# Folding the router weights two groups at a time, with the transposes of six groups behind the folds

## The chip, the cores and the metric

The kernel runs on one core of a Trainium2 chip. The metric is the device time of one execution in microseconds; smaller is better. Before the change the median of three runs is 1796.62 us (1796.1 to 1796.91).

## The reference, cut to what matters

```python
# S = 2048 tokens, D = 1024, H = 32 heads, E = 8, dk = 128
g = sigmoid((x * gate_w).sum(-1, keepdims=True))
a = attention(x, wqkv, wo)            # 32 heads, softmax, output projection
# b: a router picks one of 64 experts per token and head
q  = einsum("nd,dhc->nhc", x, w_q)    # w_q: D x 32 x 256
s1 = einsum("nhd,ed->nhe", q[..., :128], k1)
s2 = einsum("nhd,ed->nhe", q[..., 128:], k2)
e  = argmax(s1) * 8 + argmax(s2)
b  = sum over heads of gelu(x . u[e]) * v[e]
out = g * a + (1 - g) * b
```

Only the largest score of each half is asked for, so the kernel never forms `q`. It folds `w_q` with the keys into one small matrix per head and half: with `d` the model dimension, `w_q[d, head, half] . (k[e] - k[0])` for the seven differences e = 1 to 7. This folding ("router weights") is what the change touches.

## The kernel before, in words

**Stages.** The first 360 us of the span compute the queries and keys (K and Q) of the attention as a matrix product of `wqkv` and `x`, in two passes of eight units each (units 0 to 7, then 8 to 15; `KC` is 8). Units 0 and 8 are a plain product in four PSUM banks (`plain_banks`, `plain_mm`, `plain_group`, `plain_evac`); they are written out by hand and do not go through `unit(u)`. Units 1 to 7 and 9 to 15 are a Strassen-Winograd product: seven products P1 to P7 of 12 matmuls each (`product`), in the order P1, P5, P6, P2, P7, P3, P4. Every number is split into a high and a low part, and a product takes three matmuls for each of its four slices. ACT makes the high parts (`hi_of`, L138), DVE the low parts (`lo_of`, L141), the sums of the products (`add`, L519) and the sums of the weights (`w_sum`, L226) for the next unit. `evac` stores a finished K or Q block as `hi` and `lo`; what it leaves in `late` (the squares on ACT, L249, and the stores to DRAM that POOL issues) runs at the next `run_late`, which the next `evac` calls. So the square that is the last reader of a PSUM bank comes one `evac` after its block.

**The order of the work** is the order in which the code is written (a manual schedule): each engine executes its instructions in program order, and an instruction waits on semaphores for its operands and for the buffer it writes.

**Folding.** `w_q` is cut into 8 groups of 4 tiles, 32 tiles in all. One tile, one "visit", takes 4 matmuls (128 by 32 weights `kpad`, 512 columns moving, line L345); four visits of a group add up in one PSUM bank, 6 for even groups and 7 for odd ones (`bank_at(6 + gi % 2)`). `VISITS` says how many visits stand at the end of which unit, behind P4 (`fold(u)`). When a group's fourth visit is issued, ACT copies the bank to a buffer (L349, the `u7` buffer that the unit's P7 sum uses too); later four PE transposes (L360) turn it, ACT copies the result (L363, `u7` again) and POOL issues its store to `WPD` in DRAM. In the kernel before, `fold_t` does these last steps in the next unit: after P2 in units 1, 2, 8, 9 and 10 (`u % KC <= 2`), after P5 in the others. `load_wqs` loads the tiles of the next unit's visits on the SP queue: two into the `wqt` buffers, a third into an `x8` buffer.

**Banks.** The products P1 to P7 take banks 0 to 5 in turn. The plain units 0 and 8 hold their four blocks in banks 7, 0, 1 and 2; the block in bank 7 is the one with weight half 0 and column half 0.

Of the kernel before, what the change touches and what calls it, by code (L numbers as in the profile page):

```python
# [19 lines left out]
KC = D // 128  # L20
# [11 lines left out]
def gated_mha_peer_kernel(ctx, tc, xT, wqkv, wv, wo, wq, k12, ug, v, out):  # L32
# [44 lines left out]
    def dma(dst, src, queue=nc.sync):  # L77
        a, b = (ap.bitcast(F32) if ap.dtype == F32R else ap for ap in (dst, src))
        return queue.dma_start(a, b)
# [37 lines left out]
    def bank_at(i):  # L117
        return ps1.tile([128, 512], F32, name=f"bk{i}")
# [18 lines left out]
    def hi_of(parts, src):  # L137
        nc.scalar.activation(parts[0], src, AF.Copy)  # L138

    def lo_of(parts, src):  # L140
        nc.vector.tensor_tensor(out=parts[1], in0=src, in1=parts[0].bitcast(F32), op=OP.subtract)  # L141
# [63 lines left out]
    def load_w(u):  # L205
        t = wr.tile([128, 2, KC, 128], F32, name="wraw")
        for w in range(2):
            dma(t[:, w], wqkv[w * 8 + CHUNK[u]].rearrange("p (k m) -> p k m", k=KC))
        wraw[u] = raw_quarters(t)
# [9 lines left out]
    def w_sum(u, name):  # L219
        r = wraw[u]  # L220
        a, b, op, out = dict(
            S1=("A21", "A22", OP.add, None), S2=("S1", "A11", OP.subtract, "A11"),
            S3=("A11", "A21", OP.subtract, None), S4=("A12", "S2", OP.subtract, "A21"))[name]
        a, b = r[a], r[b]
        r[name] = r[out] if out else wr.tile([128, HC, 128], F32, name=name, bufs=1)
        nc.vector.tensor_tensor(out=r[name], in0=a, in1=b, op=op)  # L226

    def w_hi(u, name, src=None):
        hi_of(w_place(name), wraw[u][src or name])

    def w_lo(u, name, src=None):
        lo_of(AW[name], wraw[u][src or name])
# [9 lines left out]
    def run_late():  # L242

        for f, *a in late:
            f(*a)
        late.clear()
# [6 lines left out]
    def free_held():  # L253
        for parts, src in held:
            lo_of(parts, src)
        held.clear()

    def evac(which, c, n, src, ps, hold=False):
        hi, lo = (ev.tile([128, 512], F32R, name=part) for part in ("hi", "lo"))
        hi_of((hi, lo), src)  # L260
        run_late()
        if hold:
            held.append(((hi, lo), src))
        else:
            lo_of((hi, lo), src)
        late.append((squares, ps, src, which, c, n))
        for i, t in zip(QK_PARTS[which], (hi, lo)):
            late.append((dma, QKD[which][128 * c:128 * c + 128, i, n * 512:(n + 1) * 512], t, nc.gpsimd))
# [28 lines left out]
    def product(name):  # L297
        ps = bank_at(prod_no[0] % 6)
        prod_no[0] += 1
        a, b = (m[f] for m, f in zip((AW, X), FACTORS[name]))  # L300
        for k in range(HC):
            for i, j in ((0, 0), (0, 1), (1, 0)):
                nc.tensor.matmul(ps, a[i][:, k, :], b[j][:, k, :],  # L303
                                 start=(k == 0 and i == j == 0), stop=(k == HC - 1 and i == 1))
        return ps
# [4 lines left out]
    wq_t = {}  # L310

    def load_wq(n, third):
        t = x8.tile([128, HC, 512], F32, name="x8") if third else None
        for half in range(2):
            wq_t[n, half] = (t[:, 2 * half:2 * half + 2] if third else
                             wqp.tile([128, 2, 512], F32, name="wqt", bufs=4))
            dma(wq_t[n, half], wq[n // 4, n % 4][:, half * 1024:(half + 1) * 1024].rearrange("p (a m) -> p a m", a=2))

    VISITS = {0: 2, 1: 2, 2: 3, 3: 3, 4: 3, 5: 3, 7: 2, 8: 2, 9: 3, 10: 3, 11: 3, 12: 3}

    def load_wqs(u):
        for i in range(VISITS.get(u, 0)):
            load_wq(wq_no[0], i == 2)
            wq_no[0] += 1

    def kpad_diffs():
# [2 lines left out]
            nc.gpsimd.tensor_tensor(out=kpad[:, :, i, 7 * i:7 * i + 7], in0=kraw[:, :, 1:],  # L329
                                    in1=kraw[:, :, 0:1].to_broadcast([128, 2, 7]), op=OP.subtract)  # L330

    fold_ps, fold_no, wq_no, pending = [], [0], [0], []

    def fold(u):

        for _ in range(VISITS[u]):
            n = fold_no[0]
            fold_no[0] += 1
            gi, i = divmod(n, 4)
            if i == 0:  # L340
                fold_ps[:] = [bank_at(6 + gi % 2)]
            ps, = fold_ps
            t = wq_t.pop((n, 0)), wq_t.pop((n, 1))
            for quad in range(4):
                nc.tensor.matmul(ps[32 * quad:32 * quad + 32, :], kpad[:, quad % 2, i, :],  # L345
                                 t[quad // 2][:, quad % 2, :], start=(i == 0), stop=(i == 3))
            if i == 3:
                wt = ev.tile([128, 512], F32, name="u7", bufs=1)
                nc.scalar.activation(wt, ps, AF.Copy)  # L349
                pending.append((gi, wt))  # L350
        load_wqs(u + 2 if u == KC - 3 else u + 1)

    def fold_t():
        if not pending:
            return
        gi, wt = pending.pop(0)
        b, dh = divmod(gi, 2)
        pt = bank_at(6 + gi % 2)
        for dc in range(4):
            nc.tensor.transpose(pt[:, dc * 128:(dc + 1) * 128], wt[:, dc * 128:(dc + 1) * 128], ident)  # L360
        wt2 = ev.tile([128, 512], F32, name="u7", bufs=1)[:, :448].rearrange(
            "p (a q r) -> p a q r", a=4, q=4)
        nc.scalar.activation(wt2, pt.rearrange("p (a q r) -> p a q r", a=4, q=4)[:, :, :, :28], AF.Copy)  # L363
        dma(WPD[:, 4 * dh:4 * dh + 4, 112 * b:112 * b + 112], wt2.rearrange("p a q r -> p a (q r)"),
            nc.gpsimd)
# [82 lines left out]
    hooks = {}  # L448
# [41 lines left out]
    def unit(u):  # L490
        p, c, v = u // KC, CHUNK[u], u + 1
        n0 = TOK0[p] // 512
        seven = v < NUNIT and v != KC
        turns = (dict(P2=("S1+", "S3+", "A11"), P7=("S1", "S2+", "S2"), P3=("S4+", "A12"), P4=("S3", "S4"))
                 if u % KC == 1 else
                 dict(P1=("S1+", "S3+", "A11"), P5=("S1", "S2+"), P6=("S2", "S4+"), P2=("A12",),
                      P7=("S3",), P3=("S4",), P4=("A22",)))

        def ready(name):
            todo = turns.get(name, ()) if seven else ()  # L500
            for part in todo:
                if part[-1] == "+":
                    w_sum(v, part[:-1])
                else:
                    w_hi(v, part)
            free_held()
            for part in todo:
                if part[-1] != "+":
                    w_lo(v, part)

        def hook(name):
            for f, *a in hooks.pop((u, name), []):
                f(*a)

        def place(name):
            return ev.tile([128, 512], F32, name=name, bufs=1)

        def add(out, a, b):
            nc.vector.tensor_tensor(out=out, in0=a, in1=b, op=OP.add)  # L519

        p1 = product("P1")
        c1 = place("c1")
        nc.scalar.activation(c1, p1, AF.Copy)
        run_late()
        hook("P1")
        ready("P1")
        p5 = product("P5")
        if u % KC > 2:
            fold_t()
        hook("P5")  # L530
        ready("P5")
        p6 = product("P6")
        u2, u4 = place("u2"), place("u4")
        hook("P6")
        add(u2, c1, p6)
        add(u4, u2, p5)
        ready("P6")
        if v + 1 < NUNIT and v + 1 != KC:
            load_w(v + 1)
        p2 = product("P2")  # L540
        if u % KC <= 2:
            fold_t()
        hook("P2-")
        add(c1, c1, p2)
        evac(0, c, n0, c1, p2, True)
        hook("P2")
        ready("P2")
        p7 = product("P7")
        hook("P7-")
        u7 = place("u7")  # L550
        add(u7, u4, p7)
        add(u2, u2, p7)
        evac(1, c, n0 + 1, u7, p7, True)
        hook("P7")
        ready("P7")
        p3 = product("P3")
        hook("P3-")
        add(u4, u4, p3)
        evac(0, c, n0 + 1, u4, p3, True)
        hook("P3")  # L560
        ready("P3")
        p4 = product("P4")
        add(u2, u2, p4)
        evac(1, c, n0, u2, p4, True)
        if u in VISITS:
            fold(u)
        hook("P4")
        ready("P4")

# [26 lines left out]
    for u in range(1, KC):  # L596
        unit(u)
# [97 lines left out]
    run_late()  # L695
    rwl, rw = pools
    Wp = [(wh_[i][:, k, :], wl_[i][:, k, :]) for i in range(2) for k in range(HC)]
    assert not hooks and fold_no[0] == 32 and not pending

    blk = const.tile([128, 4], F32, name="blk")  # L700
    pr = const.tile([128, KC], F32, name="pr")
# [797 lines left out]
    for h in range(H):  # L1499
        base = h * NT  # L1500
        g, j = divmod(h, 4)
# [20 lines left out]
    for k in range(2 * KC):  # L1522
        c = slice(k % 2 * D // 2, (k % 2 + 1) * D // 2)
# [310 lines left out]
```

## Time and profile before

| | |
|---|---|
| median of 3 runs | 1796.62 us |
| the profiled execution | 1797.13 us |
| its span in the profile | 1795.4 us |
| PE busy | 1789.1 us |
| DVE, ACT, POOL busy | 1505.6, 1302.5, 264.4 us |
| matmuls of the visits (L345) | 256 records, 32.1 to 301.6 us, 31.4 us busy |
| transposes (L360) | 32 records, 4.8 us busy |

PE is TensorE's matmul stream, PEld its weight loads, DVE is VectorE, ACT is ScalarE, POOL is GpSimd, SP issues DMAs. A row of the timeline gives the start in us from the span's beginning, the duration, the engine, the line, the operation, what it writes and reads, how many in a row, and in brackets how long the engine was idle before it and what ended that. Matmuls overlap, so the time that one takes in a stream is read from start to start, not from its duration.

### The profile page before, as it was taken

Reading aid. Unit: us, or ns where it says so; the run is one execution under the profiler, and the core shown is the slowest. Engines: PE = TensorE matmul, PEld = TensorE weight load, DVE = VectorE, ACT = ScalarE, POOL = GpSimd, SP = SyncE. Lnnn points to the kernel's source line nnn. Section 1 sums busy time; section 2 is a strip of 40 time slices with the busy share of each in tenths; the row PEclk is TensorE's granted clock in tenths of the full one; section 3 lists DMA queues with packets and bytes.
Section 4 is the critical chain, followed back from the end, with each engine's and each line's share of the span. In section 5 each row is a group of like instructions: output and inputs, shape, how many; then the busy total and the mean of one; then the engine's idle time right before and its main releaser. Section 6 shows DMA issues by size and latency. Waiting matters only on the chain.

```text
span 1795.4 us, 26107 instructions
## 1 busy us (share of the span) xinstructions
PE 1789.1 (100%) x9911; PEld 1093.8 (61%) x9911; DVE 1505.6 (84%) x1295; ACT 1302.5 (73%) x1702; POOL 264.4 (15%) x395
## 2 busy tenths in 40 slices
PE   9999999999999999999999999999999999999999
PEld 7777777888888644444444444444444444447887
DVE  8866876779977898989899899989989898887874
ACT  6545544522343599999999999999999999994221
POOL 1222222244101101011101111110110111000000
PEclk9999999999999999999999999999999999999999
DMA  7887687360267668889889888988987897877541
GB/s 285 310 313 268 226 310 290 131 223 14 83 220 248 225 147 197 178 182 201 174 196 195 198 186 199 206 180 196 194 205 176 181 206 163 207 190 278 226 158 59
DMA packets 118736, 360.13 MB, mean 201 GB/s; under 512 B 16176, under 2 KB 49216, under 8 KB 95888
## 3 DMA queue, kind: packets, MB, share of 16 engines
q0 software_dynamic: 29520, 152.63, 37.1%
q1 hardware_dynamic: 87784, 203.57, 35.6%
q10 hardware_dynamic: 1304, 2.24, 0.3%
q8 instruction: 79, 1.29, 0.3%
q14 instruction: 49, 0.40, 0.1%
HBM read 171.99 MB, written 72.36 MB: 136 GB/s over the span
## 4 chain that ended last, share of the span: by engine, by line
PE 95%; DMA 2%; issue 1%; ACT 1%; DVE 0%; SPq 0%; POOL 0%; ACTq 0%; POOLq 0%; DVEq 0%
PE ring L1342 28%; PE o L1363 25%; PE bk L303 15%; PE pa L968 7%; PE bk L968 6%; PE bk L729 5%; PE bk L987 2%; PE bk L291 2%; PE bk L345 2%; DMA accd<-P 1%; PE pa L1586 1%; ACT P L1352 1%; PE ring L1376 0%; DMA rb<-rd 0%; PE bk L193 0%
## 5 line engine op out<-in xcount | busy, mean ns | idle before, releaser
L1352 ACT ACTIVATE P<-ring 128x1024 f32<-128x1024 f32 (+2 forms) x1029 | 910.0, 986 | 17.7 <-PE ring L1342 2.7
L1392 DVE TENSOR_TENSOR acc<-acc,P 128x2048 f32<-128x2048 f32 x230 | 527.0, 2291 | 34.4 <-ACT P L1352 14.6
L1363 PE MATMUL o<-P,V 128*32 128x512 f32 x3840 | 464.8, 599 | 0.0
L1342 PE MATMUL ring<-Q,K 98*128 98x512 f32 x1024 | 272.6, 408 | 0.5 <-ACT P L1352 0.5
L1342 PEld LDWEIGHTS ring<-Q,K 98*128 98x128 f32 x1024 | 182.3, 188 | 145.1 <-ACT P L1352 83.7
L1342 PE MATMUL ring<-z,z 98*128 98x512 f32 x1016 | 269.5, 407 | 0.0
L1342 PEld LDWEIGHTS ring<-z,z 98*128 98x128 f32 x1016 | 181.0, 188 | 141.4 <-ACT P L1352 76.6
L1392 DVE TENSOR_TENSOR vhl<-vhl,P 128x2048 f32<-128x2048 f32 x104 | 238.3, 2291 | 17.8 <-ACT P L1352 8.9
L1363 PEld LDWEIGHTS o<-P,V 128*32 128x32 f32 x3840 | 99.1, 109 | 222.6 <-issue 214.1
L1385 POOL DMA_DIRECT2D accd<-P x81 | 71.0, 877 | 821.3 <-ACT P L1352 412.9
L303 PE MATMUL bk<-xh,A 128*128 128x512 f32 x336 | 81.9, 394 | 0.0
L303 PE MATMUL bk<-xh,S 128*128 128x512 f32 x336 | 81.0, 392 | 0.0
L303 PE MATMUL bk<-xl,S 128*128 128x512 f32 x336 | 79.7, 390 | 0.0
L1390 DVE TENSOR_TENSOR acc<-P,P 128x2048 f32<-128x2048 f32 x22 | 50.4, 2292 | 31.7 <-ACT P L1352 31.7
L303 PEld LDWEIGHTS bk<-xh,A 128*128 128x128 f32 x336 | 62.3, 188 | 22.0 <-issue 3.4
L138 ACT ACTIVATE hi<-u 128x512 fp32r<-128x512 f32 x42 | 26.5, 632 | 65.3 <-DVE u L519 35.2
L303 PEld LDWEIGHTS bk<-xl,S 128*128 128x128 f32 x336 | 63.0, 188 | 13.0
L303 PEld LDWEIGHTS bk<-xh,S 128*128 128x128 f32 x336 | 62.6, 188 | 12.9
L968 PE MATMUL pa<-woh,acc 128*128 128x512 f32 x216 | 70.0, 390 | 0.0
L1352 ACT ACTIVATE accd<-ring 128x1024 f32<-128x1024 f32 (+2 forms) x64 | 62.3, 1033 | 0.1
L519 DVE TENSOR_TENSOR u<-u,bk 128x512 f32<-128x512 f32 x70 | 46.6, 683 | 5.3 <-DMA wpd<-u 4.5
L1395 DVE TENSOR_TENSOR acc<-acc,accd 128x2048 f32<-128x2048 f32 x22 | 50.3, 2285 | 0.0
(326 smaller groups left out, 2284.4 us busy)
## 6 DMA issues: line engine op xcount, KB each, us to landing
accd<-P POOLq DMA_DIRECT2D x81, 1024.0 KB, 9.9
wqt<-in_wq SPq DMA_DIRECT2D x48, 512.0 KB
wraw<-in_wqkv SPq DMA_DIRECT2D x28, 512.0 KB
acc<-acc POOLq DMA_DIRECT2D x19, 512.0 KB, 11.8
kd<-hi POOLq DMA_DIRECT2D x32, 256.0 KB, 3.6
kd<-lo POOLq DMA_DIRECT2D x32, 256.0 KB, 5.8
qd<-hi POOLq DMA_DIRECT2D x32, 256.0 KB, 3.6
qd<-lo POOLq DMA_DIRECT2D x32, 256.0 KB, 3.6
```

The costliest lines, as they stand in the source:

```text
L291: nc.tensor.matmul(b0[w, n], AW[PLAIN[w, ki]][a][:, k, :], X[f"B{ki + 1}{n + 1}"][b][:, k, :], start=first, stop=last)
L303: nc.tensor.matmul(ps, a[i][:, k, :], b[j][:, k, :], start=(k == 0 and i == j == 0), stop=(k == HC - 1 and i == 1))
L519: nc.vector.tensor_tensor(out=out, in0=a, in1=b, op=OP.add)
L729: nc.tensor.matmul(ps, x_part(a, t // 4, kc)[:, tok], b, start=first, stop=last)
L968: nc.tensor.matmul(ps, self.a[a][i][:, k, :], self.b[b][j][k], start=(not first and k == 0 and i == j == 0), stop=(k == HC - 1 and i == 1))
L1342: on_ring(nc.tensor.matmul(ring[:, i, :], K[:98, kt * 128:(kt + 1) * 128], Q[:98, qc * 512:(qc + 1) * 512], start=True, stop=True), i)
L1352: on_ring(nc.scalar.activation(P[h, kt][:, q0 * 512:(q0 + m) * 512].rearrange("p (a m) -> p a m", a=m), ring[:, i:i + m, :], AF.Exp, scale ...
L1363: nc.tensor.matmul(O[h][32 * qc:32 * qc + 32, :], Vt[g][:, kt, 32 * j:32 * j + 32], p[:, qc * 512:(qc + 1) * 512], start=(kt == 0), stop=( ...
L1385: nc.gpsimd.dma_start(ACCD[h], P[h, kt], accum_op=OP.add)
L1390: nc.vector.tensor_add(ACC[h], P[h, 0], P[h, kt])
L1392: nc.vector.tensor_add(ACC[h], ACC[h], P[h, kt])
L1395: nc.vector.tensor_add(ACC[h], ACC[h], ACCD[h])
```

## The change

`VISITS` now names a group (a to h) for each visit, and each half of the groups is folded in the order aa, ab, abb, bcc, ccd, ddd: the visits of two groups are open at the same time, in banks 6 and 7. The number of visits at the end of each unit is the same as before, and so is the number of loads. A group that is finished while more visits follow in the same unit (a, b, c in the first half, e, f, g in the second) is marked; its four transposes stand directly behind these visits (`fold_turn(True)`), ahead of the next unit's P1. The last `evac` of the unit, which the visits followed before, now stands behind them, and the copy of the transposed group and its store (`fold_out`) behind that `evac`. Groups d and h, which end with the last visit of a unit, are transposed in the next unit after P5. No instruction is added or removed.

```diff
-    VISITS = {0: 2, 1: 2, 2: 3, 3: 3, 4: 3, 5: 3, 7: 2, 8: 2, 9: 3, 10: 3, 11: 3, 12: 3}
+    VISITS = {0: "aa", 1: "ab", 2: "abb", 3: "bcc", 4: "ccd", 5: "ddd",
+              7: "ee", 8: "ef", 9: "eff", 10: "fgg", 11: "ggh", 12: "hhh"}
+    ALL = "".join(VISITS[u] for u in sorted(VISITS))
...
-    fold_ps, fold_no, wq_no, pending = [], [0], [0], []
+    fold_ps, fold_no, wq_no, pending = {}, [0], [0], []

     def fold(u):

-        for _ in range(VISITS[u]):
-            n = fold_no[0]
+        for left in range(len(VISITS[u]))[::-1]:
+            g = ALL[fold_no[0]]
+            gi, i = "abcdefgh".index(g), ALL[:fold_no[0]].count(g)
             fold_no[0] += 1
-            gi, i = divmod(n, 4)
             if i == 0:
-                fold_ps[:] = [bank_at(6 + gi % 2)]
-            ps, = fold_ps
-            t = wq_t.pop((n, 0)), wq_t.pop((n, 1))
+                fold_ps[gi] = bank_at(6 + gi % 2)
+            ps = fold_ps[gi]
+            t = wq_t.pop((4 * gi + i, 0)), wq_t.pop((4 * gi + i, 1))
             for quad in range(4):
                 nc.tensor.matmul(ps[32 * quad:32 * quad + 32, :], kpad[:, quad % 2, i, :],
                                  t[quad // 2][:, quad % 2, :], start=(i == 0), stop=(i == 3))
             if i == 3:
                 wt = ev.tile([128, 512], F32, name="u7", bufs=1)
                 nc.scalar.activation(wt, ps, AF.Copy)
-                pending.append((gi, wt))
+                pending.append((gi, wt, left > 0))
         load_wqs(u + 2 if u == KC - 3 else u + 1)

-    def fold_t():
-        if not pending:
+    turned = []
+
+    def fold_turn(at_once):
+        if not pending or pending[0][2] != at_once:
             return
-        gi, wt = pending.pop(0)
-        b, dh = divmod(gi, 2)
+        gi, wt, _ = pending.pop(0)
         pt = bank_at(6 + gi % 2)
         for dc in range(4):
             nc.tensor.transpose(pt[:, dc * 128:(dc + 1) * 128], wt[:, dc * 128:(dc + 1) * 128], ident)
+        turned.append((gi, pt))
+
+    def fold_out():
+        if not turned:
+            return
+        gi, pt = turned.pop()
+        b, dh = divmod(gi, 2)
         wt2 = ev.tile([128, 512], F32, name="u7", bufs=1)[:, :448].rearrange(
...
@@ unit(u) @@
         p5 = product("P5")
-        if u % KC > 2:
-            fold_t()
+        fold_turn(False)
+        fold_out()
...
         p2 = product("P2")
-        if u % KC <= 2:
-            fold_t()
...
         p4 = product("P4")
         add(u2, u2, p4)
-        evac(1, c, n0, u2, p4, True)
         if u in VISITS:
             fold(u)
+            fold_turn(True)
+        evac(1, c, n0, u2, p4, True)
+        fold_out()
```

Three places show the new order. The names: `bk6_453` is a tile in PSUM bank 6, `u7_813` one in the buffer `u7`, `wqt` and `x8` hold tiles of `w_q`; `A11`, `S4` and so on are weight parts, `xh`, `xl` parts of `x`.

PE at the end of unit 2, from the product P2 (there the kernel before transposes its first group) to P1 of unit 3, before:

```order
L303 MATMUL bk1_725<-xl0_143,A12_604 128x512 x12
L360 MATMUL bk6_738<-ident_90,u7_636 128x128 x4
L303 MATMUL bk2_754<-xh2_419,S3_649 128x512 x12
L303 MATMUL bk3_780<-xl1_144,S4_651 128x512 x12
L303 MATMUL bk4_804<-xh1_440,A22_674 128x512 x12
L345 MATMUL bk7_824<-wqt_638,kpad_131 32x512 x2
L345 MATMUL bk7_824<-wqt_640,kpad_131 32x512 x2
L345 MATMUL bk7_824<-wqt_642,kpad_131 32x512 x2
L345 MATMUL bk7_824<-wqt_644,kpad_131 32x512 x2
L345 MATMUL bk7_824<-x8_646,kpad_131 32x512 x4
L303 MATMUL bk5_852<-xh3_141,A11_681 128x512 x12
```

The same stretch of PE now:

```order
L303 MATMUL bk1_724<-xl0_143,A12_604 128x512 x12
L303 MATMUL bk2_745<-xh2_419,S3_648 128x512 x12
L303 MATMUL bk3_771<-xl1_144,S4_650 128x512 x12
L303 MATMUL bk4_795<-xh1_440,A22_673 128x512 x12
L348 MATMUL bk6_453<-wqt_631,kpad_131 32x512 x2
L348 MATMUL bk6_453<-wqt_633,kpad_131 32x512 x2
L348 MATMUL bk7_626<-wqt_635,kpad_131 32x512 x2
L348 MATMUL bk7_626<-wqt_637,kpad_131 32x512 x2
L348 MATMUL bk7_626<-x8_639,kpad_131 32x512 x4
L364 MATMUL bk6_834<-ident_90,u7_813 128x128 x4
L303 MATMUL bk5_852<-xh3_141,A11_680 128x512 x12
```

The four transposes have moved from behind P2 to behind the visits. They read `u7_813`, which ACT writes from bank 6 after the first of the three visits.

ACT at the same place, before, from the high part of P7's sum to the end of the unit (the first group's copy stands 12 rows earlier, right behind unit 1):

```order
L138 ACTIVATE hi_770<-u7_767 128x512
L249 ACTIVATE bk1_725,sq_115<-c1_669 128x512
L138 ACTIVATE S3_776<-S3_679 128x512
L138 ACTIVATE hi_794<-u4_715 128x512
L249 ACTIVATE bk2_754,sq_115<-u7_767 128x512
L138 ACTIVATE S4_800<-wraw_522 128x512
L138 ACTIVATE hi_818<-u2_714 128x512
L249 ACTIVATE bk3_780,sq_115<-u4_715 128x512
L138 ACTIVATE A22_848<-wraw_522 128x512
```

And now:

```order
L138 ACTIVATE hi_761<-u7_758 128x512
L249 ACTIVATE bk1_724,sq_115<-c1_668 128x512
L138 ACTIVATE S3_767<-S3_678 128x512
L138 ACTIVATE hi_785<-u4_714 128x512
L249 ACTIVATE bk2_745,sq_115<-u7_758 128x512
L138 ACTIVATE S4_791<-wraw_522 128x512
L352 ACTIVATE u7_813<-bk6_453 128x512
L138 ACTIVATE hi_839<-u2_713 128x512
L249 ACTIVATE bk3_771,sq_115<-u4_714 128x512
L374 ACTIVATE u7_845<-bk6_834 128x448
L138 ACTIVATE A22_848<-wraw_522 128x512
```

The copy for which the transposes wait (L352) stands behind the high part of S4, which in turn stands behind `hi_785`, the high part of P3's sum that DVE makes.

The third place is the end of unit 8, the plain unit of the second pass. PE, the last plain group and the visits, before:

```order
L291 MATMUL bk1_1768<-xl1_1716,A12_1517 128x512 x12
L291 MATMUL bk2_1769<-xl1_1716,A22_1591 128x512 x12
L345 MATMUL bk6_1748<-wqt_1757,kpad_131 32x512 x2
L345 MATMUL bk6_1748<-wqt_1759,kpad_131 32x512 x2
L345 MATMUL bk6_1748<-wqt_1761,kpad_131 32x512 x2
L345 MATMUL bk6_1748<-wqt_1763,kpad_131 32x512 x2
L303 MATMUL bk3_1993<-xh0_1646,A11_1869 128x512 x12
```

And now:

```order
L291 MATMUL bk1_1768<-xl1_1716,A12_1517 128x512 x12
L291 MATMUL bk2_1769<-xl1_1716,A22_1591 128x512 x12
L348 MATMUL bk6_1742<-wqt_1751,kpad_131 32x512 x2
L348 MATMUL bk6_1742<-wqt_1753,kpad_131 32x512 x2
L348 MATMUL bk7_1976<-wqt_1755,kpad_131 32x512 x2
L348 MATMUL bk7_1976<-wqt_1757,kpad_131 32x512 x2
L303 MATMUL bk3_1992<-xh0_1646,A11_1869 128x512 x12
```

The second visit is now the first of group f, in bank 7, which the plain unit's block `bk7_1766` held. That block's last reader is its square on ACT; around it ACT's order is, now:

```order
L138 ACTIVATE hi_1918<-bk7_1766 128x512
L249 ACTIVATE bk0_1767,sq_115<-bk0_1767 128x512
L138 ACTIVATE S3_1925<-S3_1836 128x512
L138 ACTIVATE A12_1953<-wraw_1650 128x512
L138 ACTIVATE S4_1955<-wraw_1650 128x512
L138 ACTIVATE xh3_1958<-x8_1471 128x2048
L138 ACTIVATE hi_1961<-bk1_1768 128x512
L249 ACTIVATE bk7_1766,sq_115<-bk7_1766 128x512
L534 ACTIVATE c1_2005<-bk3_1992 128x512
```

Up to that square the order is the one before; only the copy of group e (L349), which stood right behind it, has gone to the end of unit 9.

More of the change, by code (lines that the diff above doesn't have):

```diff
@@ L317, in load_wq @@
             dma(wq_t[n, half], wq[n // 4, n % 4][:, half * 1024:(half + 1) * 1024].rearrange("p (a m) -> p a m", a=2))
-    VISITS = {0: 2, 1: 2, 2: 3, 3: 3, 4: 3, 5: 3, 7: 2, 8: 2, 9: 3, 10: 3, 11: 3, 12: 3}
+    VISITS = {0: "aa", 1: "ab", 2: "abb", 3: "bcc", 4: "ccd", 5: "ddd",
+              7: "ee", 8: "ef", 9: "eff", 10: "fgg", 11: "ggh", 12: "hhh"}
+    ALL = "".join(VISITS[u] for u in sorted(VISITS))
     def load_wqs(u):
-        for i in range(VISITS.get(u, 0)):
-            load_wq(wq_no[0], i == 2)
+        for i in range(len(VISITS.get(u, ()))):
+            g = ALL[wq_no[0]]
+            load_wq(4 * "abcdefgh".index(g) + ALL[:wq_no[0]].count(g), i == 2)
             wq_no[0] += 1
@@ L697, in gated_mha_peer_kernel @@
     Wp = [(wh_[i][:, k, :], wl_[i][:, k, :]) for i in range(2) for k in range(HC)]
-    assert not hooks and fold_no[0] == 32 and not pending
+    assert not hooks and fold_no[0] == 32 and not pending and not turned
     blk = const.tile([128, 4], F32, name="blk")
```

## The prediction

> **What bounds the kernel now.** I read the page first: busy times, the chain of waits, the groups.
>
> ```profile
> PE 1789.1 (100%) x9911; PEld 1093.8 (61%) x9911; DVE 1505.6 (84%) x1295; ACT 1302.5 (73%) x1702; POOL 264.4 (15%) x395
> PE 95%; DMA 2%; issue 1%; ACT 1%; DVE 0%; SPq 0%; POOL 0%; ACTq 0%; POOLq 0%; DVEq 0%
> ```
>
> PE is busy for 1789.1 of 1795.4 us and carries 95% of the chain that ended last. Then PE's own waits over the whole trace, longest first:
>
> ```profile
> PE bk L419 <- DVE ones L74: 1.1, 1, 1.1
> ...
> PE pa L1579 <- ACT z L97: 0.2, 1, 0.2
> ```
>
> There are five, 2.7 us in all, and none of them lies between 20 and 359 us, where the changed code runs. So whatever PE gains or loses there passes on to the end: the stages behind it have no PE idle time that could take it up. The view that decides is therefore the timeline: PE first, start to start, then ACT and DVE at the places where PE would now wait for them.
>
> PE at the end of unit 2, where the kernel before transposes its first group behind P2 and makes three visits behind P4:
>
> ```profile
> 66.21 0.60 PE L360 MATMUL bk<-ident,u 128*128 128x128 f32 x4
> 66.56 3.02 PE L303 MATMUL bk<-xh,S 128*128 128x512 f32 x12
> 69.42 2.88 PE L303 MATMUL bk<-xl,S 128*128 128x512 f32 x12
> 72.14 2.88 PE L303 MATMUL bk<-xh,A 128*128 128x512 f32 x12
> 74.95 1.92 PE L345 MATMUL bk<-wqt,kpad 128*32 128x512 f32 x16
> 76.69 1.04 PE L345 MATMUL bk<-x,kpad 128*32 128x512 f32 x8
> 77.66 3.03 PE L303 MATMUL bk<-xh,A 128*128 128x512 f32 x12
> 80.53 2.88 PE L303 MATMUL bk<-xl,S 128*128 128x512 f32 x12
> ```
>
> A product takes 2.72 us (69.42 to 72.14). One ahead of visits takes 2.81, one behind them 2.87 (77.66 to 80.53). Three visits take 2.71 us, one about 0.9. Four transposes take 0.35 us and make the next product 0.14 longer (2.86): 0.49 us in the middle of a unit.
>
> **The change, part by part.** It neither adds nor removes an instruction, so PE's work stays. What can change is what PE waits for.
>
> *Term 1: group a, end of unit 2.* Its transposes wait for ACT's copy, and ACT works in order. ACT and DVE run behind PE here:
>
> ```profile
> 62.75 0.58 ACT L349 ACTIVATE u<-bk 128x512 f32<-128x512 f32 x1
> 63.23 0.62 ACT L138 ACTIVATE S<-S 128x512 fp32r<-128x512 f32 x1
> 63.88 0.69 DVE L141 TENSOR_TENSOR S<-S,S 128x512 fp32r<-128x512 f32 x1 [0.92 <-ACT S L138]
> 78.00 0.68 DVE L519 TENSOR_TENSOR u<-u,bk 128x512 f32<-128x512 f32 x1
> 78.71 0.63 ACT L138 ACTIVATE hi<-u 128x512 fp32r<-128x512 f32 x1 [1.35 <-DVE u L519]
> 79.86 0.61 ACT L138 ACTIVATE S<-wraw 128x512 fp32r<-128x512 f32 x1
> ```
>
> P3 ended by 72.4 on PE, but DVE adds it only at 78.00, and ACT's rows behind it run to the high part of S4 at 79.86. Behind that stands the new copy: ACT starts rows 0.52 us apart (62.75 to 63.23 for a copy: 0.48), so the copy would start at 80.38. The old copy at 62.75 is gone from the chain that DVE waited for at 63.88, which brings all of it 0.48 forward: copy at 79.90, done 0.58 later at 80.48. From ACT to PE and the weight load I take it from the transposes' rows:
>
> ```profile
> 105.02 0.58 PEld L360 LDWEIGHTS bk<-ident,u 128*128 128x128 f32 x4
> 105.25 0.60 PE L360 MATMUL bk<-ident,u 128*128 128x128 f32 x4
> 105.94 0.54 ACT L363 ACTIVATE u<-bk 128x448 f32<-128x448 f32 x1 [1.49 <-PE bk L360]
> ```
>
> The weight load leads by 0.23, and a hand-over between PE and ACT takes 0.09 (105.85 to 105.94). First transpose at 80.48 + 0.1 + 0.23 = 80.8, P1 of unit 3 at 80.8 + 0.35 = 81.15. Before it started at 77.66. Without the transposes behind P2 PE reaches this place earlier, but that only lengthens the wait (from about 77.2 to 80.6). Term 1 is 81.15 - 77.66 = **+3.5 us**; the ends are 3.2 (hand-over and load half as long) and 4.0 (no advance of 0.48).
>
> *Term 2: group f, end of unit 8.* Its first visit writes bank 7, which holds the plain block until ACT has squared it:
>
> ```profile
> 172.72 0.69 DVE L519 TENSOR_TENSOR u<-c,bk 128x512 f32<-128x512 f32 x1 [4.15 <-PE bk L303]
> 210.77 1.92 PE L345 MATMUL bk<-wqt,kpad 128*32 128x512 f32 x16
> 212.63 3.06 PE L303 MATMUL bk<-xh,A 128*128 128x512 f32 x12
> 216.03 0.57 ACT L138 ACTIVATE hi<-bk 128x512 fp32r<-128x512 f32 x1
> 216.50 0.59 ACT L249 ACTIVATE bk<-bk 128x512 f32<-128x512 f32 x1
> 217.02 0.19 ACT L249 ACTIVATION_READ_ACCUMULATOR bk<-bk 128x1 f32 x1
> ```
>
> By ACT's order the square of bank 7 is the one at 216.50. It is done at 217.09, with its accumulator at 217.21. PE is ready for f's first matmul at 210.77 + 0.93 = 211.70. So PE waits until 217.21 + 0.1, **+5.6 us**; the ends are 5.4 (released at 217.09) and 5.9 (a weight load on top). Does ACT get there earlier? DVE last waited for PE at 172.72 and both engines are busy from there, with nothing changed between; the place moves with PE as a whole, and term 1 cannot eat it up. In the first pass the same clash has room: there the plain block is squared in unit 1, before b's first visit.
>
> *Term 3: the other four or five.* For b, c, e, f and g the transposes leave the middle of a unit (-0.49) and stand behind the visits: 0.35, the 0.14 at the next product's start, minus the 0.15 that the product behind visits paid, plus the step from visits to transposes, which no row shows. Nearest is that 0.15, also a step from 32 to 128 columns; with it the move is free, and without any step it saves 0.15 each. [...] I take -0.06 each, -0.3 in all. Do they wait? With two visits behind the group (b, e, f) 1.8 us cover a copy of 0.58. With one (c, g) the group ends about T + 1.92 (T the start of the visits), the copy T + 2.6, the first load T + 2.7, where PE arrives at T + 2.71: 0 to 0.2 each. ACT must be there in time:
>
> ```profile
> 96.94 1.92 PE L345 MATMUL bk<-wqt,kpad 128*32 128x512 f32 x16
> 97.62 0.61 ACT L138 ACTIVATE S<-wraw 128x512 fp32r<-128x512 f32 x1
> 119.08 0.61 ACT L138 ACTIVATE S<-wraw 128x512 fp32r<-128x512 f32 x1
> 119.43 1.92 PE L345 MATMUL bk<-wqt,kpad 128*32 128x512 f32 x16
> 231.37 1.28 DVE L519 TENSOR_TENSOR u<-u,bk 128x512 f32<-128x512 f32 x2 [4.39 <-DMA wpd<-u]
> 232.43 1.92 PE L345 MATMUL bk<-wqt,kpad 128*32 128x512 f32 x16
> 237.01 0.61 ACT L138 ACTIVATE A<-wraw 128x512 fp32r<-128x512 f32 x1
> ```
>
> In units 3 and 4 ACT's row ahead of the copy is done (98.2, 119.7) when PE ends the group (98.0, 121.4) or just behind it, and term 1 gives it 3.5 us more. In unit 9 it would be late (237.01), but DVE's wait of 4.39 for the store from `u7` goes, since no transposed group sits there now; that takes it to 232.6, and term 2 delays PE further. This wait was off PE's path, so its end gains nothing by itself. If it stayed and term 2 did not come, e would cost about 3.8. Ends of term 3: -0.75 and +0.9.
>
> *At no cost.*
>
> ```profile
> L79 POOL DMA_DIRECT2D wpd<-u x8: 757/758/767, 70.7 to 309.2; - x8
> L79 SPq DMA_DIRECT2D wpl<-wpd x2: 319/350/380, 305.7 to 315.4; - x2
> ```
>
> The copies of the turned groups and their stores stand behind the last `evac`, so the store of 0.76 us on POOL's queue stands behind stores that are ready sooner; the data is not read before 305 us. That `evac` now waits on ACT behind the copy: its high part comes 1 to 3 us later at most, and DVE's row on it too; the next reader of those two engines' results on PE is a unit away. SP's loads keep their number and places; behind term 2 they are issued later, with PE itself that much later.
>
> **Sum.** 3.5 + 5.6 - 0.3 = +8.8 us. The profiled execution took 1797.13 (span 1795.4 and 1.7 around it), 0.5 above the median; put on the median of 1796.62 this gives **1805.4**. What a measurement of this kernel can tell from no change is about 0.2%, 3.6 us.
>
> **Rivals.** *Half pace behind the wait.* At the start of the span PE fills its time with equal matmuls:
>
> ```profile
> 1.06 1.83 PE L419 MATMUL bk<-fill 128*112 128x112 f32 x8 [1.06 <-DVE ones L74]
> 4.07 0.95 PE L419 MATMUL bk<-fill 128*112 128x112 f32 x8
> ```
>
> Eight take 1.83 us, and 3 us later 0.95: PE starts at half pace. If the 5.3 us of idling in unit 8 bring that back for 3 us, half of them are lost: +1.5, up to +3.0 if it lasts twice as long, so about 1807.4. Against it: no idle time of more than 1.1 us occurs in this trace, so no row shows a return. [...]
>
> *The bank is free in time* (the not-slower case). If f's first matmul had to wait only for the high part, or ACT squared bank 7 before 212, only term 1 stays: 1796.6 + 3.5 - 0.3 = 1799.8, no change. It decides the sign once the wait falls under 0.4 us. Against it: the square writes the bank, and the row stands 4.8 us behind PE.
>
> *ACT catches up in unit 2*, so that term 1 goes: 1796.6 + 5.6 - 0.3 = 1801.9. For it speaks only the 0.48 of the removed copy; it would take 3.5.
>
> *No waits at all:* the edges alone, 1796.3 (with term 3 at its end 1795.9).
>
> **How the numbers follow.** Forecast 0.48, with a range of its own from 1804.3 to 1806.6; half pace 0.30; unit 8 alone 0.06; unit 2 alone 0.08; no waits 0.05; more than all this 0.03. The range from 1801.6 to 1808.8 leaves out unit 2 alone, no waits and more: 0.16. Slower: 0.48 + 0.30 + 0.06 + 0.03 = 0.87. Same: 0.08 and most of 0.05, 0.11. Faster: 0.02.
>
> **What would show it.** In the new trace: PE idle for 3.4 us ahead of the first transposes (L364), released by ACT's copy (L352); PE idle for 5.5 us ahead of the visits of unit 8 (L348), released by ACT's square (L249); no other PE idle above 0.3 us before 360 us; DVE's 4.39 us wait for the store gone; products at 2.72 us behind the long wait, or twice that for some 3 us if the half pace returns. It is wrong if PE shows no wait in unit 8, or if a later stage takes the loss back.

## The result, and the profile after

The changed kernel takes 1808.28 us (median of 6 runs, 1807.47 to 1810.18); the kernel before, in the same runs, 1796.43. The ratio is 1.0062, with a 95% interval from 1.0043 to 1.0082: slower by 11.85 us. The forecast was 1805.4 with a range from 1801.6 to 1808.8. The time lies in the range, but nearer to the rival with half pace (1807.4) than to the forecast, and 0.5 us from the range's upper end.

The page of the changed kernel, busy times and chain:

```profile
PE 1791.2 (99%) x9911; PEld 1095.4 (61%) x9911; DVE 1506.1 (83%) x1295; ACT 1303.4 (72%) x1702; POOL 264.3 (15%) x395
PE 93%; DVE 1%; issue 1%; ACT 0%; DVEq 0%; ACTq 0%
```

PE's busy time has grown by 2.1 us with the same 9911 matmuls, and PE is idle for longer: the span is 1805.6 and not 1795.4. PE's own waits, longest first (in all, times, longest):

```profile
PE bk L348 <- ACT bk L249: 5.4, 1, 5.4
PE bk L364 <- ACT u L352: 3.1, 1, 3.1
PE bk L430 <- DVE ones L74: 1.1, 1, 1.1
```

The first two are new, and they are the two that terms 1 and 2 named, with the releasers that they named. The end of unit 2 in the timeline, PE:

```profile
74.87 1.92 PE L348 MATMUL bk<-wqt,kpad 128*32 128x512 f32 x16
76.61 1.04 PE L348 MATMUL bk<-x,kpad 128*32 128x512 f32 x8
80.78 0.66 PE L364 MATMUL bk<-ident,u 128*128 128x128 f32 x4 [3.12 <-ACT u L352]
81.19 2.98 PE L303 MATMUL bk<-xh,A 128*128 128x512 f32 x12
```

ACT there:

```profile
79.63 0.61 ACT L138 ACTIVATE S<-wraw 128x512 fp32r<-128x512 f32 x1
80.15 0.57 ACT L352 ACTIVATE u<-bk 128x512 f32<-128x512 f32 x1
```

The copy stands behind the high part of S4, as ACT's order said, and PE waits for it. The weight load of the first transpose starts 0.01 us ahead of its matmul:

```profile
80.77 0.42 PEld L364 LDWEIGHTS bk<-ident,u 128*128 128x128 f32 x4 [4.03 <-ACT u L352]
```

The copy ends at 80.72; first transpose at 80.78 (forecast 80.8), P1 of unit 3 at 81.19 (forecast 81.15). The end of unit 8, PE:

```profile
214.05 1.07 PE L348 MATMUL bk<-wqt,kpad 128*32 128x512 f32 x8
220.52 1.94 PE L348 MATMUL bk<-wqt,kpad 128*32 128x512 f32 x8 [5.40 <-ACT bk L249]
222.38 4.66 PE L303 MATMUL bk<-xh,A 128*128 128x512 f32 x12
226.88 5.62 PE L303 MATMUL bk<-xh,S 128*128 128x512 f32 x24
```

And ACT, the square of bank 7:

```profile
219.77 0.59 ACT L249 ACTIVATE bk<-bk 128x512 f32<-128x512 f32 x1
220.28 0.18 ACT L249 ACTIVATION_READ_ACCUMULATOR bk<-bk 128x1 f32 x1
```

Group f's first matmul starts at 220.52, right behind the square's second row, the read of its accumulator (220.46), and 5.54 us behind the place where PE was ready (214.05 + 0.93). What follows is slow: one visit takes 1.86 us and not 0.93, and the product behind it 4.50 (222.38 to 226.88) and not 2.89. The windows around it say why (PE busy, number of matmuls, granted TensorE clock as a share of full speed, DMA share, GB/s):

```profile
214.00:218.00 4.00, 1.12 (x9) 1.00 0.86 280
218.00:222.00 4.00, 1.48 (x8) 0.64 0.84 309
222.00:223.00 1.00, 1.00 (x6) 0.50 0.62 254
...
225.00:226.00 1.00, 1.00 (x4) 0.53 0.61 172
226.00:227.00 1.00, 1.00 (x6) 1.00 0.99 311
```

The granted clock falls to 0.50. From the shares in the two mixed windows, 2.88 us of the four from 218 and 0.94 of the one from 225, the slow stretch runs from 219.12 to 225.94: 6.82 us. Half of that, 3.41 us, is the window of which the expectations below speak.

**Where the time went**, in the two profiled executions (1797.13 and 1807.47 us): 3.1 us in unit 2 (P1 of unit 3 came 3.5 us later, but 0.4 of that was there before: PE's visits of unit 0 began at 32.55 and not 32.13); 5.5 us of waiting in unit 8; 2.5 us of half pace behind it (0.93 + 1.61); and -0.45 at the edges, 0.09 for each of five groups. Their sum is 10.7. With the later start this is the 11.1 us by which the stage behind the last unit begins later (370.96 and not 359.87). The spans differ by only 10.2. The rest of the kernel took 1434.6 us here and 1435.5 before; over the ten profiles of this document it took 1434.2 to 1435.7, and 1434.5 where nothing was lost ("both edits" below). So this is spread between executions, not a loss taken back.

### The profile page after: what moved, and what is told of

The parts are those of the page before. It is cut to its first block, busy times and chain, and to the rows that moved or that the text cites. A ratio compares the mean times of both kernels' runs of the same rounds, so it can differ in the third digit from the quotient of the medians.

```text
span 1805.6 us, 26098 instructions
## 1 busy us (share of the span) xinstructions
PE 1791.2 (99%) x9911; PEld 1095.4 (61%) x9911; DVE 1506.1 (83%) x1295; ACT 1303.4 (72%) x1702; POOL 264.3 (15%) x395
## 3 DMA queue, kind: packets, MB, share of 16 engines
q8 instruction: 79, 1.29, 0.3%
## 4 chain that ended last, share of the span: by engine, by line
PE 93%; DVE 1%; issue 1%; ACT 0%; DVEq 0%; ACTq 0%
PE ring L1353 29%; PE o L1374 26%; PE bk L303 12%; PE pa L979 7%; PE bk L979 6%; PE bk L740 5%; PE bk L998 2%; PE pa L1590 1%; PE bk L348 1%; PE pa L1597 1%; PE ring L1387 0%; DVE xh L141 0%; DVE x L155 0%; PE bk L364 0%; ACT xh L138 0%
## 5 line engine op out<-in xcount | busy, mean ns | idle before, releaser
L141 DVE TENSOR_TENSOR lo<-u,hi 128x512 fp32r<-128x512 f32 x42 | 29.0, 692 | 24.8 <-ACT hi L138 23.5
```

## The experiments

Each has its ratio to the kernel before on the same chip. The first four ran together (before: 1796.83), the last four together (before: 1796.19).

**f begins in unit 9.** Term 2 taken away, term 1 left.

```diff
-              7: "ee", 8: "ef", 9: "eff", 10: "fgg", 11: "ggh", 12: "hhh"}
+              7: "ee", 8: "ee", 9: "fff", 10: "fgg", 11: "ggh", 12: "hhh"}
```

> The second half of the groups is visited in the order ee, ee, fff, fgg, ggh, hhh: group f begins in unit 9, so nothing writes bank 7 behind unit 8; e is transposed in unit 9 after P5. Theory (PE waits for the square of bank 7, and its half pace comes from that idle time): the 5.4 us wait and the 2.5 us of half pace both go, granted clock 1.000, about 8 us less than the changed kernel: 1800.2 us. Rival (the loss behind unit 8 comes from the moved last evac or from the order of the loads, which stay as changed): 1808 us, with the wait and the slow stretch still there. Rival two (half pace has another cause than the wait): 1802.8 us, the wait gone and the clock still below 1.

Measured: 1800.63 us (1799.73 to 1802.91), ratio 1.0021 [1.0012, 1.0031], 7.7 us less than the changed kernel's 1808.28; against the kernel before, the loss falls from 11.85 to 3.80 us. The wait of unit 8 is gone. But the clock is not 1.000 as expected: it reads 1.000 in two of the ten runs and 0.998 or 0.999 in the others, and the profile shows why. PE at the end of unit 2:

```profile
76.24 1.04 PE L348 MATMUL bk<-x,kpad 128*32 128x512 f32 x8
80.43 1.12 PE L364 MATMUL bk<-ident,u 128*128 128x128 f32 x4 [3.16 <-ACT u L352]
81.20 5.43 PE L303 MATMUL bk<-xh,A 128*128 128x512 f32 x12
86.47 2.90 PE L303 MATMUL bk<-xl,S 128*128 128x512 f32 x12
```

And its windows (PE busy, matmuls, granted clock, DMA share, GB/s), of which the first and the last of the slow ones:

```profile
79.00:80.00 1.00, 0.00 (x0) 0.82 0.92 311
80.00:81.00 1.00, 0.57 (x3) 0.50 0.95 307
...
86.00:87.00 1.00, 1.00 (x5) 0.77 1.08 336
```

Here the wait of 3.16 us in unit 2 halved the clock too, from 79.64 to 86.46 (again 6.82 us), and P1 of unit 3 took 5.27 us. In the changed kernel's profile the same wait of 3.12 did not.

**a is turned in unit 3.** Term 1 taken away, term 2 left.

```diff
-                pending.append((gi, wt, left > 0))
+                pending.append((gi, wt, left > 0 and gi != 0))
```

> Group a alone is not turned behind the visits of unit 2 but in unit 3 after P5; all else as changed, the copy of a stays where it is. Theory (PE waits 3.1 us for ACT's copy): that wait goes, the clash in unit 8 and the half pace stay: 1805.2 us. Rival (the copy ahead of the last evac holds up ACT and DVE and that is what costs): no gain, 1808 us. In unit 3 DVE may wait for the store from the shared buffer; that costs PE nothing by the theory.

Measured: 1803.27 us (1802.26 to 1805.55), ratio 1.0036 [1.0024, 1.0049]. The wait of unit 2 is gone, that of unit 8 is 5.4 us as before, clock 0.998 or 0.999 in every run. PE's waits, longest first:

```profile
PE bk L348 <- ACT bk L249: 5.4, 1, 5.4
PE bk L430 <- DVE ones L74: 1.1, 1, 1.1
```

The copy still stands ahead of the last evac, so the rival falls. The gain is 5.0 us (5.4 if each version is set against the kernel before of its own group of runs), where 3.1 was expected. Half pace in unit 2, which the wait there can bring (see the experiment above), would account for the rest; no trace shows it in the changed kernel itself, so this part is argued.

**Both edits.**

> Both edits together: f begins in unit 9, a is turned in unit 3 after P5. Theory: no PE wait above 0.3 us before 360 us, clock 1.000; b, c, f and g behind their visits save 0.1 us each at the edges: 1796.0 us, which is the kernel before within what can be told. Rival (two groups open at a time cost something by themselves): above 1798 us.

Measured: 1796.20 us (1795.18 to 1797.33), ratio 0.9997 [0.9987, 1.0006], clock 1.000 in all ten runs. PE's waits in full:

```profile
PE bk L430 <- DVE ones L74: 1.1, 1, 1.1
PE bk L740 <- ACT xu L744: 0.3, 1, 0.3
PE bk L291 <- ACT xh L399: 0.3, 1, 0.3
```

With the two waits gone, nothing that these runs can tell is left of the loss: by the interval, two open groups, the moved evac and the moved stores together cost at most 1.1 us. The gain at the edges, 0.4 us for four groups, is below what these runs can tell. This is the best version found, and it is not measurably faster than the kernel before.

**PE kept busy in unit 8.**

```diff
             if i == 0:
+                if gi == 5:
+                    spare = bank_at(prod_no[0] % 6)
+                    for _ in range(20):
+                        nc.tensor.matmul(spare[:112, :112], warm, warm, start=True, stop=True)
                 fold_ps[gi] = bank_at(6 + gi % 2)
```

> The changed kernel with 20 small matmuls of constants (128 by 112, about 4.7 us at full pace, result never read) between e's and f's visits in unit 8, where PE idles. Theory (the half pace comes from idling for more than one window): the wait shrinks to under 1 us, the end of the wait stays where it was, granted clock 1.000 and products at 2.72 us at once: 2.5 to 3.5 us less than the changed kernel, 1805.3 us. Rival (the slow stretch has another cause, such as loads of weights or memory traffic at that place): clock still 0.5 for some us, 1808 us.

Measured: 1806.09 us (four runs, 1804.52 to 1806.88), ratio 1.0051 [1.0034, 1.0068]. PE in unit 8 (each of the 20 matmuls stands as two records):

```profile
216.00 4.19 PE L347 MATMUL bk<-fill 128*112 128x112 f32 x40
221.47 1.07 PE L352 MATMUL bk<-wqt,kpad 128*32 128x512 f32 x8 [1.29 <-ACT bk L249]
222.47 3.02 PE L303 MATMUL bk<-xh,A 128*128 128x512 f32 x12
```

And the windows at the wait's end:

```profile
221.00:222.00 1.00, 0.53 (x8) 1.00 0.82 332
222.00:223.00 1.00, 1.00 (x10) 1.00 0.73 295
```

The visit behind the wait takes 1.00 us and the clock stays at 1.00. The same instructions at the same place, with the same loads under way, run at full pace if PE has idled for 1.29 us and not for 5.40: the half pace there comes from the idle time. Three expected numbers were missed: the wait is 1.29 us and not under 1, the gain 2.2 us and not 2.5 to 3.5, and the clock of the whole run is 0.999 in three of the four runs. In the profiled one, the wait of unit 2 (3.29 us) halved the clock for 3.4 us.

**The square of bank 7 earlier**, on the version with a turned in unit 3.

```diff
     plain_evac(KC, 0, 0)
+    run_late()
```

> On the version that turns group a in unit 3 (so only the wait of unit 8 is left): the square of the plain block in bank 7 is issued directly behind its high part, five ACT rows earlier. It must still wait for DVE's low part of that block, so f's first matmul comes about 2.0 us late and not 5.4. Theory: wait 2.0 us, too short to halve the clock (1.000 in every run): 1796.8 - 0.4 + 2.0 = 1798.4 us. Rival (any wait of PE halves the clock): wait 2.0 us and clock 0.998 to 0.999, above 1800 us. Rival two (the wait is for something else than this square): 1803 us.

Measured: 1799.73 us (1797.47 to 1804.49), ratio 1.0019 [1.0009, 1.0028]. PE in unit 8:

```profile
210.72 1.06 PE L348 MATMUL bk<-wqt,kpad 128*32 128x512 f32 x8
213.78 1.06 PE L348 MATMUL bk<-wqt,kpad 128*32 128x512 f32 x8 [1.99 <-ACT bk L249]
214.77 4.59 PE L303 MATMUL bk<-xh,A 128*128 128x512 f32 x12
```

ACT there, the square:

```profile
213.03 0.58 ACT L249 ACTIVATE bk<-bk 128x512 f32<-128x512 f32 x1 [2.11 <-DVE lo L141]
213.53 0.20 ACT L249 ACTIVATION_READ_ACCUMULATOR bk<-bk 128x1 f32 x1
```

And PE's windows behind it:

```profile
215.00:216.00 1.00, 1.00 (x4) 0.61 0.84 229
216.00:217.00 1.00, 1.00 (x4) 0.50 1.06 422
217.00:218.00 1.00, 1.00 (x4) 0.50 1.06 410
218.00:219.00 1.00, 1.00 (x5) 0.69 0.95 369
```

The wait shrank from 5.4 to 1.99 us with the square that releases it, as expected. That it was too short to halve the clock was wrong: the clock is 0.5 from 215.22 to 218.62 (3.40 us), and 7 of 10 runs show 0.998 or 0.999. The three runs that kept 1.000 took 1797.47 to 1798.08 us, the other seven 1798.76 to 1804.49.

**The copy of a earlier on ACT**, on the version with f in unit 9; unit 2 alone.

```diff
         add(u4, u4, p3)
+        if u == 2:
+            run_late()
+            p4 = product("P4")
+            fold(u)
         evac(0, c, n0 + 1, u4, p3, True)
```

(P4 and the visits are then left out at their old place in that unit.)

> On the version that begins f in unit 9 (so only the wait of unit 2 is left): in unit 2 alone the product P4 and the visits are issued ahead of P3's evac, so that ACT's copy of group a stands ahead of the high parts of P3's sum and of S4, behind the square of P7's sum. Theory (the transposes wait for what stands ahead of the copy on ACT): copy at about 77.5 us and not 80.1, wait 1.0 to 1.3 us and not 3.2, no half pace: 1797.6 us. Rival (the wait comes from the visits or the bank itself): wait unchanged, 1800.6 us.

Measured: 1796.68 us (1796.06 to 1797.40), ratio 1.0002 [0.9992, 1.0011], clock 1.000 in all ten runs. ACT:

```profile
77.10 0.60 ACT L352 ACTIVATE u<-bk 128x512 f32<-128x512 f32 x1
77.76 0.63 ACT L138 ACTIVATE hi<-u 128x512 fp32r<-128x512 f32 x1
```

And PE:

```profile
77.75 0.66 PE L364 MATMUL bk<-ident,u 128*128 128x128 f32 x4 [0.95 <-ACT u L352]
```

Moved ahead of two high parts on ACT, the copy starts at 77.10 and not 79.81 as in the version it is built on, and the wait falls from 3.16 to 0.95 us. So the wait of term 1 was set by the copy's place in ACT's order; what stood ahead of it includes the first high part's own wait of 1.36 us for DVE's sum of P3. At 0.95 us no run lost its clock.

**A shorter idle time in unit 8**, on the version with a turned in unit 3: the small matmuls again, but 13 of them.

```diff
             if i == 0:
+                if gi == 5:
+                    spare = bank_at(prod_no[0] % 6)
+                    for _ in range(13):
+                        nc.tensor.matmul(spare[:112, :112], warm, warm, start=True, stop=True)
                 fold_ps[gi] = bank_at(6 + gi % 2)
```

> On the version that turns group a in unit 3: 13 small matmuls of constants (about 2.7 us) between e's and f's visits in unit 8, so that PE idles for about 2.6 us there and not 5.4; the end of the wait stays where it is. Theory A (the clock halves when a window of 3.41 us is mostly idle; seen at 69% idle, not seen at 47%): some runs keep 1.000 and some show 0.999, 1802.3 to 1804 us, below 1803.3 on the median. Theory B (a whole idle window is needed): clock 1.000 in all runs, 1802.0 us.

Measured: 1802.69 us (five runs, 1801.66 to 1804.32), ratio 1.0035 [1.0021, 1.0049]. PE in unit 8:

```profile
216.91 1.07 PE L352 MATMUL bk<-wqt,kpad 128*32 128x512 f32 x8 [2.67 <-ACT bk L249]
```

Four of the five runs show 0.999, and one, the profiled one, 1.000. That fits theory A and not B: a wait of 2.67 us is shorter than a window of 3.41. The 47% in A is the author's estimate: no trace marks a window where the clock stays whole. The trace here is of the run that kept its clock; a fall without 3.41 us of idling is seen in the traces of "f begins in unit 9" (3.16) and "the square of bank 7 earlier" (1.99). The time is no further help here, since it is the end of the wait that decides and only the half pace differs.

**The changed kernel once more.**

> The changed kernel once more, beside the others on one chip: 1808.3 us, clock 0.996 to 0.998; half pace behind unit 8 in every run, behind unit 2 in some. The profile shows half pace in stretches of 3.4 or 6.8 us.

Measured: 1808.23 us (four runs, 1806.47 to 1810.50), ratio 1.0069 [1.0052, 1.0085], clock 0.997 or 0.998. In its profile the waits are 5.41 and 3.10 us; the clock is halved for 6.8 us behind unit 8 and not at all in unit 2. Half pace in unit 2 in some runs, as expected, is thus not seen in a trace of this kernel.

## Why the prediction was right or wrong

*What bounds.* Right: PE had no slack, and both waits reached the stage behind the last unit in full; no later stage took them back.

*Term 1 (3.5 us): the wait was right, its size 0.4 too large.* The net loss was 3.1 us. Most of the difference is the step from the end of ACT's copy to the first transpose: the sum put 0.33 there, 0.23 of it for the weight load, and it took 0.06. Measured from PE's start, ACT also reached the copy 0.2 us sooner than forecast, and the transposes took 0.06 longer. That P1 of unit 3 came within 0.04 us of its forecast place is luck: this execution started 0.4 us later, and ACT moved with PE (in the four profiles with this wait the first transpose comes 48.2 to 48.4 us behind the first visit of unit 0). Half the hand-over and load, which the prediction gives as its end of 3.2, makes 3.3 by its own numbers.

*Term 2 (5.6 us): right.* 5.54 us; released at the accumulator's end, as assumed. With f begun later the wait is gone, with the square earlier it shrinks to 1.99 us.

*Term 3 (-0.3 us): right in sign.* The step that no row showed costs 0.06 on the transposes, which take 0.41 us behind visits and 0.35 behind a product; the changed kernel at the end of unit 3:

```profile
102.16 1.04 PE L348 MATMUL bk<-x,kpad 128*32 128x512 f32 x8
103.13 0.66 PE L364 MATMUL bk<-ident,u 128*128 128x128 f32 x4
103.54 3.02 PE L303 MATMUL bk<-xh,A 128*128 128x512 f32 x12
106.40 2.88 PE L303 MATMUL bk<-xl,S 128*128 128x512 f32 x12
```

So the step behind visits, 0.15 ahead of a product, is only 0.06 ahead of a transpose; 0.09 is saved for each group, -0.45 in all. The forecast's -0.06 for each was the author's choice between 0 and -0.15; the runs show -0.09 and not that. Groups c and g did not wait: of the forecast 0 to 0.2 each it was 0. (The prediction's upper end for this term, +0.9, is not worked out there; the waits that it names make 0.4.)

*The covers: right.* DVE's 4.39 us wait for the store is gone, and no other PE wait appeared. That e was in time is shown with term 2 present only; with f in unit 9 e moves too, so the price of 3.8 us was not tried.

*The half pace: the step that failed.* It stood among the rivals at 0.30 and for unit 8 alone; it was there in every run of the changed kernel (0.996 to 0.998 in the six runs). The sum should have carried it: 2.5 us in the profiled execution, where the rival said 1.5 to 3.0. All 41 runs of the kernel before that stand beside the experiments read 1.000. And it was not counted for unit 2. Yet the wait there, of 3.1 to 3.3 us, halved the clock in two of the four profiles that have it (f later and PE kept busy) and left it whole in the other two (the changed kernel's both).

*The sum.* Without half pace the waits and the edges made 8.2 us where the forecast was 8.8. The measured 11.85 lies in the range because the range was drawn to hold the rival; the prediction's most likely case, the two waits at full pace, did not come. That the time still fell 0.5 us inside is in part luck: the 3.7 us that are left for the half pace are more than the rival's 3.0, and waits smaller than forecast made up for 0.6 of it.

*What stays open.* The waits and the edges make 8.2 us of the 11.85 between the medians; 3.7 is left for the half pace. With one wait alone the same subtraction leaves 1.1 (f later: 3.8 - 3.1 + 0.4) and 1.3 (a later: 6.4 - 5.5 + 0.4), 2.4 together. The granted clock of the changed kernel's runs, 0.996 to 0.998, stands for 7 to 14 us at half pace. Seven of its ten runs read 0.996 or 0.997, which is more than the 6.8 us of the profiles, while no run with the wait of unit 8 alone read below 0.998. So these seven probably had slow stretches at both places; no trace of such a run was taken. Whether the last 1.3 us is that or the spread of the runs (4 us) is not settled.

## What to carry to other kernels

Where PE is the bound, moving an operation next to its producer is worth what its edges cost (here 0.09 us) and can cost what stands ahead of the producer on its own engine (here a wait of 3.12 us): follow the order of the engine that feeds it, not the distance in the code. A buffer that is taken earlier waits for its old owner's last reader, which may be a deferred one (here 5.40 us); look up that reader's place before a bank is reused sooner. And price a new PE wait with the half pace that may come behind it: it came here behind waits of 1.99 to 5.41 us, and took another 1.6 to 2.8 us in the profiles that have it.

## What the runs showed of the hardware

In the six profiles that show it, the clock was halved for 3.4 us (the square earlier and PE kept busy) or 6.8 us (the changed kernel's both, f later, a turned in unit 3). The fall came 4.0 us behind the start of PE's idle time in the changed kernel's profile (219.12 and 215.12), 2.4 us behind it with f later (79.64 and 77.28), and with the square earlier 1.4 us behind its end (215.22 and 213.78), when PE was busy again.

In the 3.41 us ahead of these three falls PE was idle for all of the time (the changed kernel, unit 8), for 2.36 us (f later: 77.28 to 79.64) and for 1.97 (square earlier: 211.81 to 213.78, 58%). So the fall did not take 3.41 us of idling without a break. Nor did the length of the wait decide alone: one of 3.12 us (the changed kernel, unit 2) left the clock whole, one of 1.99 (square earlier) did not. What else decided is not shown.

By the granted clock of the runs, with the length of the wait taken from the profiled one: the wait of 0.95 us lost the clock in none of ten runs, that of 1.99 us in 7 of 10, that of 2.67 in 4 of 5, that of 3.16 (f later) in 8 of 10, and that of 5.40 (a turned in unit 3) in all six.

The half clock lasted longer where PE was still idle at the fall: 6.82 us in the changed kernel's profile (fall at 219.12, PE busy from 220.52) and with f later (79.64, busy from 80.43). Where PE was already busy it lasted 3.4 us: with the square earlier (215.22, busy from 213.78) and in unit 2 with PE kept busy in unit 8 (80.60, busy from 80.15).
